# Six steps' output products of the fifth token group put off behind the last group's first layer

## The chip, the cores and the metric

The kernel runs on one core of a Trainium2 chip. The metric is device time in microseconds (us), lower is better. Three runs of the kernel before took 541.68 us in the median (541.45 to 542.41). Five engines work side by side: TensorE (PE, with its weight loads shown as PEld), VectorE (DVE), ScalarE (ACT), GpSimd (POOL), and SyncE (SP), whose queue issues the DMAs here.

## The reference

Three layers follow each other on 4 batches of 768 positions (3072 tokens of 256 values):

```python
x = attn(x, a, B, C)                                  # decay attention, chunked scan over 768 positions
h = np.maximum(np.maximum(x @ w1, x @ w2), x @ w3)    # first expert layer, 256 -> 768
x = h @ w_out                                         # 768 -> 256
h = x @ w_in                                          # second expert layer, 256 -> 2048
P = a[0] + a[1] * h + a[2] * h * h + a[3] * h * h * h
Q = 1.0 + abs(b[0]) * abs(h) + abs(b[1]) * h * h
out = (P / (Q + 1e-6)) @ w_out2                       # 2048 -> 256
```

Everything is fp32. A factor that is not exact in TensorE's fast format is split into two parts, hi and lo, and a product then takes three passes.

## The kernel before, in words

The 3072 tokens go in NG = 6 groups of T = 512 tokens (128 positions of each of the 4 batches). Each group goes through attention, the first expert layer and the second. The second is cut into 16 steps of 128 of the 2048 hidden values; step g.k below is step k of group g, both counted from 0, so the fifth group's steps are 4.0 to 4.15 and the last group's 5.0 to 5.15.

One step, written by `h_plan`, is this:

- **First layer.** Six passes of 512 columns on PE (two halves of the 256 inputs, each hi by hi, lo by hi, hi by lo; lines 856 to 858 in `mm3`) fill one PSUM bank. Called H5.4 for step 5.4.
- **Rational function.** Some 12 operations on tiles of 128x512. ACT reads the bank for `Abs` (line 1058) and a linear term (line 1056), and takes Ln and Exp (1074, 1075); POOL makes a linear term and a product (1042, 1060); DVE does the rest (1061, 1062, 1076, 1079, 1081). A second form has Square, Abs and a linear term on ACT (1065, 1066, 1069); a third, used in the last group only, copies the bank and has two products on POOL (1047 to 1053). Each works in slots A4 to A12 of SBUF; the odd steps of the last group work in slots H0 to H11, which held the first expert layer's hidden values.
- **Split.** ACT rounds the result to hi (line 1086, through the helper at line 374), POOL subtracts for lo (line 1087). Three slots each: A13 to A15 and A16 to A18.

`o_plan` then has two output products (O4.10 means both of step 4.10), three passes each, which add up over the 16 steps of a group in the two PSUM banks S2 and S3. Steps 5.6 to 5.15 use an unsplit fp32 product instead (line 1105). At the end of a group the banks are copied out and sent by DMA (lines 1123 and 1124; 1117 and 1118 for the very last step, which is done in two halves).

What sets the order: the kernel records every operation with what it reads, writes and which slot it needs, and then issues the operations engine by engine in the order of a list. That list comes from a greedy scheduler (`listed`), which reads one number per operation from a packed table, `KEYS`. Each engine runs its own list strictly in order, waiting on semaphores where an operand is not ready or a slot not free. DMAs stand in SP's list in the same way.

Of the kernel before, what the change touches and what calls it, by code (L numbers as in the profile page):

```python
# [10 lines left out]
F32 = mybir.dt.float32  # L11
F32R = mybir.dt.float32r
# [5 lines left out]
DR = bass.MemoryType.DRAM  # L18
# [6 lines left out]
T = NB * CH  # L25
# [12 lines left out]
OHALF, G0L, SPLIT = True, False, 6  # L38
# [40 lines left out]
class Plan:  # L79
# [255 lines left out]
def decay_attention_max_moe_rational_moe(  # L335
# [121 lines left out]
    def mark():  # L457
        return _Tile()
# [763 lines left out]
```

## Time and profile before

| | us |
|---|---|
| median of 3 runs | 541.68 (541.45 to 542.41) |
| the profiled execution | 541.84 |
| its span, first to last instruction | 539.70 |
| outside the span | 2.14 |
| mean granted clock of PE | 0.999 of full speed |

The profile is of one execution. Its page gives the busy time of each engine as a share of the span; views of the trace give the same in any window, the rows of one engine in order of time, and the chain of waits, followed back from the last instruction. In a row of an engine's timeline a bracket such as [0.56 <-ACT A L1058] is the time that the engine was idle before the row, and what ended it. An operation's printed duration on ACT, DVE and POOL can reach a little into the next one's, and so can a pass on PE (0.39 us printed, a start every 0.23 us).

### The profile page before, as it was taken

How to read it: one execution, taken by the hardware profiler on the slowest of the kernel's cores; microseconds unless marked ns; L12 is line 12 of the kernel's file. 1: busy time of each engine (PE TensorE's matmuls, PEld its weight loads, DVE VectorE, ACT ScalarE, POOL GpSimd, SP SyncE). 2: the span in 40 equal slices, each digit the busy share in tenths (PEclk: the TensorE clock that was granted, in tenths of full speed). 3: DMA queues.
4: the chain of work that ended last, by engine and by line, in shares of the span. 5: the costliest groups of instructions: out<-in, count | busy, mean ns of one | idle time of the engine just before them, and what ended most of it. 6: DMA issues, size and time to landing. Idle time of an engine off the chain costs nothing.

```text
span 539.7 us, 8473 instructions
## 1 busy us (share of the span) xinstructions
PE 529.9 (98%) x2866; PEld 413.9 (77%) x2866; DVE 488.5 (91%) x763; ACT 446.5 (83%) x772; POOL 435.5 (81%) x418
## 2 busy tenths in 40 slices
PE   9899999999999999999999999999999999999987
PEld 4466678888888888888888788888888888887743
DVE  6898999876987999999998999999989899789997
ACT  6998876747766998898988899989688788789994
POOL 1366557788888999998988889998878888689994
PEclk9999999999999999999999999999999999999999
DMA  6687844432624100010030100030000100001001
GB/s 217 222 294 259 242 151 158 151 112 85 239 99 149 60 20 1 0 40 1 1 117 0 40 2 1 0 125 12 1 1 1 39 2 0 2 1 39 1 0 39
DMA packets 17413, 39.46 MB, mean 73 GB/s; under 512 B 3123, under 2 KB 4443, under 8 KB 17371
## 3 DMA queue, kind: packets, MB, share of 16 engines
q1 hardware_dynamic: 17371, 38.94, 21.4%
q8 instruction: 22, 0.36, 0.3%
q14 instruction: 20, 0.16, 0.1%
HBM read 30.13 MB, written 8.80 MB: 72 GB/s over the span
## 4 chain that ended last, share of the span: by engine, by line
PE 87%; DVE 4%; DMA 3%; ACT 3%; SPq 1%; issue 1%; DVEq 0%; ACTq 0%
PE S L856 14%; PE S L858 14%; PE S L857 14%; PE G L856 7%; PE G L858 7%; PE G L857 7%; PE D L856 5%; PE D L858 5%; PE D L857 5%; PE S L1105 3%; PE Y L747 2%; DMA R<-in_w_dram 1%; PE S L699 1%; SPq L463 1%; DMA A<-in_bn_dram 1%; PE G L715 1%
## 5 line engine op out<-in xcount | busy, mean ns | idle before, releaser
L1087 POOL TENSOR_TENSOR A<-A,A 128x512 fp32r<-128x512 f32 x83 | 108.4, 1308 | 16.4 <-ACT A L374 15.8
L1060 POOL TENSOR_TENSOR A<-A,A 128x512 f32<-128x512 f32 x65 | 85.0, 1309 | 3.3
L1074 ACT ACTIVATE Y<-A,qc 128x512 f32<-128x512 f32 (+1 forms) x89 | 61.4, 690 | 11.8 <-POOL A L1060 8.2
L856 PE MATMUL S<-A,L 128*128 128x512 f32 x172 | 67.1, 390 | 0.2 <-ACT A L374 0.2
L857 PE MATMUL S<-A,L 128*128 128x512 f32 x172 | 67.1, 390 | 0.0
L1079 DVE SCALAR_TENSOR_TENSOR Y<-A,co,Y 128x512 f32<-128x512 f32 (+1 forms) x89 | 66.6, 748 | 0.4
L858 PE MATMUL S<-A,L 128*128 128x512 f32 x172 | 67.0, 389 | 0.0
L1076 DVE SCALAR_TENSOR_TENSOR A<-A,Y 128x512 f32<-128x512 f32 (+1 forms) x89 | 60.4, 679 | 7.1 <-ACT Y L1075 6.9
L428 POOL TENSOR_TENSOR C<-C,E 128x256 uint32<-128x256 uint32 x56 | 43.7, 796 | 25.0 <-DVE C L423 19.4
L1081 DVE SCALAR_TENSOR_TENSOR A<-A,Y 128x512 f32<-128x512 f32 (+1 forms) x89 | 60.6, 681 | 1.8
L374 ACT ACTIVATE A<-A 128x512 fp32r<-128x512 f32 x83 | 52.3, 630 | 10.6 <-DVE A L1081 6.7
L1042 POOL TENSOR_SCALAR A<-A,co 128x512 f32<-128x512 f32 (+1 forms) x69 | 55.6, 805 | 5.0 <-ACT A L1058 4.6
L1075 ACT ACTIVATE Y<-Y 128x512 f32<-128x512 f32 (+1 forms) x97 | 56.2, 581 | 2.1
L475 POOL TENSOR_TENSOR H<-X,H 128x512 fp32r<-128x512 f32 x30 | 40.2, 1342 | 10.4 <-ACT H L374 10.3
L856 PE MATMUL G<-xhi,w_hi 128*128 128x512 f32 x120 | 46.8, 390 | 0.0
L858 PE MATMUL G<-xhi,w_lo 128*128 128x512 f32 x120 | 46.7, 389 | 0.0
L857 PE MATMUL G<-xlo,w_hi 128*128 128x512 f32 x120 | 46.7, 389 | 0.0
L856 PEld LDWEIGHTS S<-A,L 128*128 128x128 f32 x172 | 32.3, 188 | 7.4 <-ACT A L374 0.7
L857 PEld LDWEIGHTS S<-A,L 128*128 128x128 f32 x172 | 32.3, 188 | 7.3 <-POOL A L1087 0.7
L858 PEld LDWEIGHTS S<-A,L 128*128 128x128 f32 x172 | 32.3, 188 | 6.7
L1056 ACT ACTIVATE A<-S,co 128x512 f32<-128x512 f32 x38 | 29.6, 779 | 3.7 <-POOL A L1087 2.1
L1071 POOL TENSOR_TENSOR A<-A,A 128x512 f32<-128x512 f32 x20 | 26.0, 1298 | 7.3 <-DVE A L1067 6.2
(247 smaller groups left out, 1561.4 us busy)
## 6 DMA issues: line engine op xcount, KB each, us to landing
R<-in_wo_dram SPq DMA_DIRECT2D x11, 512.0 KB
R<-in_w_dram SPq DMA_DIRECT2D x9, 512.0 KB
R<-in_win_dram SPq DMA_DIRECT2D x8, 512.0 KB
L<-in_xn_dram SPq DMA_DIRECT2D x6, 512.0 KB
out_dram<-A SPq DMA_DIRECT2D x10, 256.0 KB
xt_d<-L SPq DMA_DIRECT2D x4, 512.0 KB
L<-xt_d SPq DMA_DIRECT2D x4, 512.0 KB
y_d<-A SPq DMA_DIRECT2D x8, 256.0 KB
```

What stands on the lines that cost most here:

```text
L374: act.activation(out=o, in_=i, func=AF.Copy)
L856: pe.matmul(dst, wh, hi, start=first, stop=False, skip_group_check=skip)
L857: pe.matmul(dst, wh, lo, start=False, stop=False, skip_group_check=skip)
L858: pe.matmul(dst, wl, hi, start=False, stop=last, skip_group_check=skip)
L1042: pop(0.74, lambda: pool.tensor_scalar(out=f(t1), in0=f(v), scalar1=c(5), scalar2=c(4), op0=ALU.mult, op1=ALU.add), [v], [t1])
L1060: pop(1.26, lambda: pool.tensor_tensor(out=f(v), in0=f(t1), in1=f(v), op=ALU.mult), [t1], [v])
L1074: aop(0.6, lambda: act.activation(out=f(r), in_=f(v), func=AF.Ln, bias=qc), [v], [r])
L1075: aop(0.49, lambda: act.activation(out=f(r), in_=f(r), func=AF.Exp, scale=-1.0), [], [r])
L1076: dop(0.6, lambda: dve.scalar_tensor_tensor(out=f(v), in0=f(v), scalar=QC, in1=f(r), op0=ALU.add, op1=ALU.mult), [r], [v])
L1079: dop(0.67, lambda: dve.scalar_tensor_tensor(out=f(r), in0=f(w), scalar=c(0), in1=f(r), op0=ALU.add, op1=ALU.mult), [w], [r])
L1081: dop(0.6, lambda: dve.scalar_tensor_tensor(out=f(w), in0=f(v), scalar=2.0, in1=f(r), op0=ALU.subtract, op1=ALU.mult), [v, r], [w])
L1087: pop(1.26, lambda: pool.tensor_tensor(out=f(lo), in0=f(w), in1=f(hi).bitcast(F32), op=ALU.subtract), [w, hi], [lo])
```

## The change

A new constant DEFER = 6 names the last six steps of the fifth group, 4.10 to 4.15. Their hi and lo, once made, are each written to a DRAM tile (12 writes of 256 KB, line 1096 after the change) and read back (12 reads, line 1098) into slots of the H ring, and the output products read the copies that came back. For each step the slots A13 to A18 come free when the write has landed, not when the products are done. No instruction of PE, ACT, DVE or POOL is added or removed; SP gets 24 DMAs more. The table `KEYS` is a new one for all operations (`ZERO` goes with it, the number that is subtracted from each entry), so the whole order is written anew.

```diff
-OHALF, G0L, SPLIT = True, False, 6
+OHALF, G0L, SPLIT, DEFER = True, False, 6, 6
...
-    LOOK, KEEP, SCALE, ZERO = 0.2, 1.5, 97.0, 0.0
+    LOOK, KEEP, SCALE, ZERO = 0.2, 1.5, 97.0, 7.0
     KEYS = (
-        "XaLOv2LUnxDgeX*3j+B8I{+{NVgmUBoC0+M8UkGcT?76Dm;<r{-2<`)*94&jc?Kf{%m;P|s{lI(BF-+-xdLzn-UV+3xCOHYAPB(-=?EM"
...
+        "SOOFVg#o_=E&$;H83h0ZIRw)I5(OOvTm|?9+yoT`4hEwJC<bx{q6XLrc?a|dAPKhySPCTzSpu~QzR#@DX$2Puh6w2gUkF+W{t9pllnbH"
...
+    g_d = [dram.tile([2, 128, T], F32, name=f"g_d{k}") for k in range(DEFER)]
...
-        return hi, lo
+        if g < NG - 2 or last or k < F2 - DEFER:
+            return hi, lo
+        back = hhi_r((128, T), F32R), hlo_r((128, T), F32R)
+        d, there = g_d[k - F2 + DEFER], [mark() for _ in range(2)]
+        for i, z in enumerate((hi, lo)):
+            op("dma", 0.35, lambda i=i, z=z: nc.sync.dma_start(out=d[i], in_=z.t.bitcast(F32)), [z], [there[i]], size=262.0)
+        for i, z in enumerate(back):
+            op("dma", 0.35, lambda i=i, z=z: nc.sync.dma_start(out=z.t.bitcast(F32), in_=d[i]), [there[i]], [z],
+               when["h", (NG - 1) * F2] - 2.0 + 2 * (k - F2 + DEFER), size=262.0)
+        return back
```

Line numbers after the change are higher by 2 up to the split, and by 11 in `o_plan`.

PE around the last group's steps 5.0 to 5.4, before. The number in front is the instruction's place in PE's list. S2 and S3 are the banks of the output products, A13 to A18 hold hi and lo of the fifth group's results, K0 to K3 the last group's input to the layer, G_5562 is the bank of step 5.4:

```order
2276 L856 MATMUL S2_5027<-A13_5435,L4_2333 128x512
2277 L857 MATMUL S2_5027<-A16_5446,L4_2333 128x512
2278 L858 MATMUL S2_5027<-A13_5435,L4_2333 128x512
2279 L856 MATMUL S3_5036<-A13_5435,L4_2333 128x512
2280 L857 MATMUL S3_5036<-A16_5446,L4_2333 128x512
2281 L858 MATMUL S3_5036<-A13_5435,L4_2333 128x512
2282 L856 MATMUL S2_5027<-A14_5475,L4_2333 128x512
2283 L857 MATMUL S2_5027<-A17_5487,L4_2333 128x512
2284 L858 MATMUL S2_5027<-A14_5475,L4_2333 128x512
2285 L856 MATMUL G_5562<-K0_5375,win_hi_98 128x512
2286 L857 MATMUL G_5562<-K1_5383,win_hi_98 128x512
2287 L858 MATMUL G_5562<-K0_5375,win_lo_99 128x512
```

The products of steps 4.12 and, in part, 4.13 stand ahead of H5.4. The same engine and place after the change, where G_5573 is the bank of step 5.4, S1_5541 that of 5.3, and H1 and H6 hold what was read back for step 4.11:

```order
2267 L858 MATMUL S1_5541<-K2_5444,win_hi_104 128x512
2268 L859 MATMUL S1_5541<-K3_5470,win_hi_104 128x512
2269 L860 MATMUL S1_5541<-K2_5444,win_lo_105 128x512
2270 L858 MATMUL S2_5052<-H1_5479,L3_2270 128x512
2271 L859 MATMUL S2_5052<-H6_5502,L3_2270 128x512
2272 L860 MATMUL S2_5052<-H1_5479,L3_2270 128x512
2273 L858 MATMUL S3_5060<-H1_5479,L3_2270 128x512
2274 L859 MATMUL S3_5060<-H6_5502,L3_2270 128x512
2275 L860 MATMUL S3_5060<-H1_5479,L3_2270 128x512
2276 L858 MATMUL G_5573<-K0_5366,win_hi_104 128x512
2277 L859 MATMUL G_5573<-K1_5377,win_hi_104 128x512
2278 L860 MATMUL G_5573<-K0_5366,win_lo_105 128x512
```

H5.4 now stands behind the products of 4.11, at place 2276 in place of 2285.

ACT at the end of the fifth group, before (in the same order of names: A15 and A13 get hi of steps 4.14 and 4.15, G_5562 is the bank of step 5.4, D_5520 that of 5.3):

```order
691 L374 ACTIVATE A15_5548<-A7_5419 128x512
692 L1074 ACTIVATE Y1_5539<-H1_5546,qc_108 128x512
693 L374 ACTIVATE A13_5560<-A8_5465 128x512
694 L1056 ACTIVATE H2_5569<-D_5520,co_89 128x512
695 L1058 ACTIVATE H3_5575<-D_5520 128x512
696 L1075 ACTIVATE Y1_5539<-Y1_5539 128x512
697 L1056 ACTIVATE A7_5584<-S1_5506,co_89 128x512
698 L1058 ACTIVATE A4_5590<-G_5562 128x512
699 L1056 ACTIVATE A8_5598<-G_5562,co_89 128x512
```

Seven instructions stand between hi of 4.14 (691) and the Abs of step 5.4 (698). The same after the change, where A13 and A14 get hi of 4.14 and 4.15, G_5573 is the bank of step 5.4, D_5506 that of 5.1:

```order
686 L376 ACTIVATE A13_5551<-A7_5453 128x512
687 L1076 ACTIVATE Y0_5556<-A5_5521,qc_114 128x512
688 L1077 ACTIVATE Y0_5556<-Y0_5556 128x512
689 L376 ACTIVATE A14_5570<-A8_5476 128x512
690 L1068 ACTIVATE Y1_5580<-D_5506,co_95 128x512
691 L1060 ACTIVATE A4_5590<-G_5573 128x512
692 L1058 ACTIVATE A7_5598<-S0_5524,co_95 128x512
693 L376 ACTIVATE A15_5602<-A9_5515 128x512
694 L1058 ACTIVATE A8_5611<-G_5573,co_95 128x512
```

The Abs of step 5.4 now stands at place 691, where hi of 4.14 stood, and both hi copies stand ahead of it.

SP's list after the change, where g_d3, g_d4 and g_d5 are the DRAM tiles of steps 4.13, 4.14 and 4.15 (before, none of these rows is there):

```order
144 L1096 DMA g_d4_91<-A13_5551 128x512
145 L1098 DMA H8_5568<-g_d3_90 128x512
146 L1096 DMA g_d5_92<-A14_5570 128x512
147 L1096 DMA g_d4_91<-A16_5582 128x512
148 L1098 DMA H1_5600<-g_d4_91 128x512
149 L1096 DMA g_d5_92<-A17_5592 128x512
150 L1098 DMA H2_5619<-g_d5_92 128x512
```

The read of lo of 4.13 (145) stands behind the write of hi of 4.14 (144) in the queue.

## Rows read from the trace of the kernel before

**Rows 1.** Page, busy time, share and instructions of each engine.
```profile
PE 529.9 (98%) x2866; PEld 413.9 (77%) x2866; DVE 488.5 (91%) x763; ACT 446.5 (83%) x772; POOL 435.5 (81%) x418
```

**Rows 2.** 20-us windows: length, busy PE, PEld, DVE, ACT, POOL, clock, DMA share, GB/s.
```profile
460.00:480.00 20.00, 20.00 (x90) 16.57 (x89) 15.01 (x24) 15.30 (x26) 15.21 (x14) 1.00 0.01 2
480.00:500.00 20.00, 19.77 (x88) 15.94 (x87) 19.69 (x31) 19.59 (x36) 18.45 (x17) 1.00 0.07 26
500.00:520.00 20.00, 18.32 (x74) 13.50 (x74) 18.77 (x30) 19.06 (x33) 19.60 (x19) 1.00 0.00 1
520.00:540.00 20.00, 16.65 (x50) 7.93 (x48) 15.98 (x29) 11.53 (x24) 12.29 (x14) 0.96 0.08 26
```

**Rows 3.** The chain of waits from 483 us: start us, us, what.
```profile
483.68 0.24 PE S L858
...
483.94 0.60 ACT A L1058
...
505.17 0.69 DVE H L1061
...
513.65 0.67 DVE A L1053
...
514.37 0.50 PE G L856
...
536.73 0.42 DVE A L376
```

**Rows 4.** Timeline of PE, the last group's first layer: start us, us.
```profile
480.80 0.39 PE L858 MATMUL G<-K,win_lo 128*128 128x512 f32 x1
...
487.82 0.39 PE L856 MATMUL G<-K,win_hi 128*128 128x512 f32 x1
...
488.96 0.39 PE L858 MATMUL G<-K,win_lo 128*128 128x512 f32 x1
```

**Rows 5.** Timeline of ACT, end of the fifth group and after.
```profile
481.24 0.60 ACT L1058 ACTIVATE A<-G 128x512 f32<-128x512 f32 x1
...
482.58 0.60 ACT L1065 ACTIVATE H<-S 128x512 f32<-128x512 f32 x1
483.08 0.78 ACT L1069 ACTIVATE H<-S,co 128x512 f32<-128x512 f32 x1
...
486.13 0.64 ACT L374 ACTIVATE A<-A 128x512 fp32r<-128x512 f32 x1
...
487.34 0.63 ACT L374 ACTIVATE A<-A 128x512 fp32r<-128x512 f32 x1
...
490.20 0.60 ACT L1058 ACTIVATE A<-G 128x512 f32<-128x512 f32 x1
...
503.82 0.83 ACT L1056 ACTIVATE H<-S,co 128x512 f32<-128x512 f32 x1
```

**Rows 6.** Timeline of DVE, the first operation of step 5.9 on it.
```profile
505.17 0.69 DVE L1061 TENSOR_TENSOR H<-S,H 128x512 f32<-128x512 f32 x1 [0.83 <-ACT H L1058]
```

**Rows 7.** Timeline of POOL, waits before the last group and POOL's last operation.
```profile
470.37 2.66 POOL L1087 TENSOR_TENSOR A<-A,A 128x512 fp32r<-128x512 f32 x2 [3.26 <-ACT A L374]
...
482.01 0.77 POOL L1042 TENSOR_SCALAR A<-A,co 128x512 f32<-128x512 f32 x1 [0.52 <-ACT A L1058]
...
484.72 0.77 POOL L1042 TENSOR_SCALAR A<-A,co 128x512 f32<-128x512 f32 x1 [0.56 <-ACT A L1058]
...
532.21 0.73 POOL L1052 TENSOR_TENSOR A<-A,A 128x256 f32<-128x256 f32 x1
```

**Rows 8.** Timeline of SP's queue, a write to DRAM and the read behind it.
```profile
134.93 1.05 SPq L968 DMA_DIRECT2D y_d<-A  x2
137.59 0.32 SPq L979 DMA_DIRECT2D A<-y_d  x1
```

**Rows 9.** The chain of waits at 38 us: a 256 KB load under load.
```profile
38.58 5.43 DMA A<-in_bn_dram
```

**Rows 10.** Window of 4 us with that load, columns as in rows 2.
```profile
40.00:44.00 4.00, 3.94 (x76) 2.84 (x76) 3.25 (x8) 3.99 (x8) 1.69 (x3) 1.00 1.00 330
```

More of the change, by code (lines that the diff above doesn't have):

```diff
@@ new lines @@
+        "IxD&?g)HJN4lRf;YB3-#d@sy1a51zkpD@5LATJOxr!ILfnlk<|KQxUp{V}>SiZfI(>@f#2?l7w}4>8#|_cQ7<{xilkr8dMfh%-GlEjIx"
+        ";4mjdCNdue%<pk*hg$0rbQweYhX$%JqmkkFB)CtrHi3xBES_nA_N(s9Lr2^OmxCVL$Q3n47;0JaG_69}=mj^!x=>~uYJO~2`rUoJiNea"
+        ";m0t}T3?g#e=-Uww1#t1VAZwlWDQV4_z@(I2QhY9ZqrV9BA9195yxC?v?LJeRL>l0=XWDXAx8V?~6@(@iCWeVvEehX#{To3yV{0)>2S_"
+        "=dWF$@t6atyBxRSnh*-3)CF4h<{~!wotM;|#M7st%+MD-Wy@NfN#izz)$3fDP6Shz-~cX$>w9@(#Ka9S=SZ_zrLn4iT^r?-J$`ZV_P+y"
+        "Al%<-4o&yHW7>ug%8OPYY-<85E7^oi4P$Umk+EEoezBv+YqV{+7OQr!Ve}8FcM)Aoe}jAT@cg~-4c@(U=|@4I}`2^K@eOKI1*P9!V<O<"
@@ new lines @@
+        "jS{aCO%gd1mJ{F;A{5yZ+7(9@0vX{HITb(^FBk_Jc^9`9suh+Msudp>0~2l&;TK~RV-u7U;1t6Xt`ubz_7hwb&=#f?!xiBbUlf29aTQ<"
+        "`JrocYkQ-eb>K!B$lNk6F4i_XC0~qrb92cw?7Z}zSdKa-67a3U@85+(Uj~nS8@fxff?iuqRUmr9X_ZY+(eHmIBaUHuG*Bp)-WEKb+uNs"
+        "jUF&R=D1Q{?I<QhB~=NZcybsFOu^cwpYsvE!_8X!d>9wD6@&KsT@%Ni#gup2@eBp=`#;2pmmM;*i*k{m@JG9EY~)gdQ0ZygyO=p3dWf*"
+        "-9P>>l48$sVj9`5piqogg707$CtO#vptlI3x5RaUMz@4I|MXR3O|ZW+B@kLMap^wjmQM9V-4P_&1?C6G;U(B{#G;bvU#)0y%d%f;xXXr"
+        "#l2X4LRC40Xio-<~dtBv^#`4V>{tK#X!qCaXo`P+dB6<dqD|2A3(7{RzAT%Jw2{F)IB{x+&vjRR6xx?2tWoxPeFx2NI!-_mOytx=0eLt"
@@ new lines @@
+        "s6r1y1x71H4@S5~R74X*l|%VP&_&%v8Aj4Z#7DhJ`$>XIlSRr#6-bmvCr8akYD^eQF-z1-$V&lD|3=wKs!NGZ`%DZ_{ZMC7Yf&Uuepr5"
+        "8Xb^i6R~4lf02iYc`We9)z!;Dj#2Q)}l_5SLjv>|`ej^4Vxgs$n3?ZE(?jvL*up#Cn7bK}9<|ObXRU|ehlO&lY=Os%giYHMi_$T}(p(j"
+        "8o^(R3owI|mqaw#?{uPDkYYbv)XjVZP%aV!2Te=3qI`YeYlm@A1Z*etFsdnc_Z7%3VlEiI)jSS^<=MlLTdY%G#5A}t&+0WLW%^)Rw6S2"
+        "1)g(k?GB9x*R4^)7}mVliMbxiZc%Co<+Us4=cFa5O$Ltue<jzB2<eB{V%UHa6ijh%ibt{4wh>d^aaGW;fk6pf}<)Wi_idKQ_=efj7)J>"
+        "^N^a(l(PfP&n{5xH*tGQ#vR*^g>@nDl(lkBQ#bvPB<_*syfy=c{`yxP(4~bx;j)k0z23|AUs<<(mW_VnLyDz%RF{HPCS`A<UplCen96w"
@@ new lines @@
+        "$3Ct;$Ui|sK0=T}<3Ue9qCp@*2||%V^FdTY%R{a}mqFb^m_wdJs6^C3B}QsQ4MuQARYbBz2Sy`D)<=Fu3rB-PIYxs;wnvahb4P?mgGio"
+        "9Wk~cm*f<h6Y&ZotJvx6n(m8rP5<FHura$FLSV%KW14?Z;+&C&aQ#xTg(K??yBSqIl^F=a7fkv)M6-uH?_eoAW07BnCCqTGD2SEry`a+"
+        "jORzlB2@kQ-PkxQ9Mh)jb;I7v`N^+S?K0!qS4X-LdSr%6>y@JcOB2}}u1MNSP#Z%S-Naz@WbAWX(fBue^A$w?wj@=PgB<V{>n%S|mww@"
+        "fxn`b@-3(o8N*PEGwwIZS6wZB6-2cTmw#lTT+zt4sb&woMXGl})2h8&9cE>rdoQdr$;W0#eXX%~AbJXH5l8^G<M2IZi52T2LoYUr}gK@"
+        "KF9y&rx_&P*eR(`%f88`A&LJZBZ&wQc>Jd3{t&OQ&THZe^U)r2UV3%*iisd!%|96s#5w@%Th#AlT)QrPE%i1F;<gR99KwBq*Gi}4^yU8"
@@ new lines @@
+        "g~)Tr*2xpeV8&d?P0A0*_sI3hg~@x$sLF`SzsPXP+sGTq(#k-^dc*F;*Tp8qeZ(=x-^aSfu*ieRs>qkgP0iiMC%`So;=-H7kjE#+f5(l"
+        "+*2hW5aL6Faf6U*?*vwJIC&vuN4#>U9HOV*0jLAjIP|J16@5@}uA<ccntjLMRf5|b+vB}iRsmmG3I?L6{!OZ^3l+J0%C&@g>vdO#0I?E"
+        "EwThHUmpUj-f8q6Wk6VFD^A;+l6HO<${lg#MI)Xd||`O6Z{Y0l=$-p<v~k<anU|I4||FU(iXInDCXywPOO=gdUTY0nhTZOy{UWX_Jt!p"
+        ")D&3Cyd`*vt9NiPx*rz0cXt7Sq_wsLepnfzRU3)XhrIh|a#xSJZ&eS<hn9g3YMUNXrw`)y)&pTF&~;BGPZxQqD5Z&DR;ukkI?oGSG$5q"
+        "SoHcOwvEjHqcYjR@#=%o6cU>=h3RpP0<+EBGu2<Gt{!vpw*euu+aV1")
```

102 lines of the change are left out of this document (39 added, 63 removed).

## The prediction

> **What bounds the kernel now.** I read the page's first part first: PE is busy for 529.9 of 539.7 us, ACT, DVE and POOL for 81 to 91% [rows 1]. An average says little here, so next come the windows of 20 us where the change lies. PE is full in 460 to 480, 0.23 us short in 480 to 500, 1.68 us short in 500 to 520; in the same two windows DVE, ACT and POOL have 19.69, 19.59, 18.45 and then 18.77, 19.06, 19.60 us of 20 [rows 2]. So the bound moves from PE to the other three near 480 us. The chain of waits says the same: it lies on PE until 483.92, then on ACT and DVE until 514.32, then on PE, which after 514.37 does the last products one behind the other [rows 3]. Between 484 and 514 us what counts is therefore when the operations of the rational function get through ACT, DVE and POOL, and PE only as far as it feeds them.
>
> **What the change removes and adds.** It removes nothing. It adds 24 DMAs of 256 KB on SP's queue, and it moves instructions on all engines. In the first 480 us PE is full or nearly so and keeps its passes; the swaps there I put at 0 (bounds −0.4 and +0.4 us, about two passes, since each moves an operation past one or two others).
>
> **Term 1, PE.** Its work is the same, so it gains only what it stood still for: at most 0.23 + 1.68 = 1.91 us [rows 2]. It would earn that if the other three engines were fed earlier and could use it. H5.0 to H5.3 come three places earlier, 0.68 us, and H5.4 nine places earlier (2276 for 2285). A pass takes 0.227 us (H5.4's first and sixth stand 1.14 us apart [rows 4]), so H5.4 starts at 487.82 − 2.04 = 485.78 and ends, as before, 1.53 us later (488.96 + 0.39 − 487.82 [rows 4]): 487.31.
>
> **Term 2, ACT, on which my forecast rests.** In ACT's list the Abs of step 5.4 moves further than H5.4 does: it takes the place that hi of 4.14 had before, and that began at 486.13 [rows 5]. Its bank is not full by then. The nearest handover of this kind is H5.0, whose last pass ends at 480.80 + 0.39 = 481.19 [rows 4], and its Abs began at 481.24 [rows 5], 0.05 later. So the Abs of 5.4 can start at 487.36, not at 486.13: ACT, which runs its list in order, stands for up to 1.23 us, and 30 further instructions stand behind it up to the linear term of step 5.9. Before, the 31 instructions from hi of 4.14 on took 503.82 − 486.13 = 17.69 us [rows 5], with at most 20 − 19.59 = 0.41 us idle in that window [rows 2]. After, the 31 are the same but that two hi copies (0.64 + 0.63) went ahead and the Square and linear term of step 5.1 (0.60 + 0.78 [rows 5]) came in: +0.11. With 0.30 of the idle time gone (between none and 0.41), 487.36 + 17.69 + 0.11 − 0.30 = 504.86 us, where before it was 503.82: +1.04 (from +0.93 to +1.34).
>
> What stands behind that: DVE's first operation of step 5.9 waited 0.83 us for ACT before and began at 505.17 [rows 6], 1.35 us behind the linear term; now at 506.21. From there on the lists of ACT, DVE and POOL are nearly as before, and the chain runs through DVE to 514.32 [rows 3]. DVE's own idle time between 500 and 520 was 20 − 18.77 = 1.23 us [rows 2], of which 0.83 is this wait, so 0.40 is left to take some of it up. The end moves by +0.64 to +1.04; I take +0.7, near the lower end, because the DVE operations ahead of step 5.9 get the longer wait to catch up in.
>
> **Term 3, POOL.** It has about one operation of work behind another from 484.72 to 532.94 (532.21 + 0.73). The waits that earlier first layers can take away are 0.52 at 482.01 and 0.56 at 484.72, both for an Abs of the last group's first steps [rows 7]: −1.08 at best. The product of step 5.1 gets a new wait in their place, since 5.1's linear term on ACT now stands behind the Abs of 5.4. Net I take 0, which leaves term 2 to decide.
>
> **Term 4, the DMAs.** Issuing them is SP's work and covered. What can cost is a read that comes late for PE. The last tight one is lo of step 4.13. Its read is queued behind the write of hi of 4.14, which ACT makes behind the Abs of 5.2: H5.2's last pass (place 2263, nine after H5.0's last at 480.80) ends at 483.23, Abs and hi copy take 0.60 and 0.64 [rows 5], the write's issue about 0.5 (1.05 for two [rows 8]): 485.0. O4.13 is due on PE at 488.5 (place 2288, 34 passes behind 480.80). A write of 256 KB and the read behind it stood 2.66 us apart in the trace (134.93 to 137.59 [rows 8]): by that the copy is there at 487.7, in time, cost 0. A 256 KB load took 5.43 us on the chain [rows 9] in a stretch where the DMA engines were busy through whole windows [rows 10]: by that it is there at 490.4, and PE stands 1.9 us. I take 0, because the 12 writes and 12 reads, 6.3 MB in some 23 us, are about 270 GB/s, below the 330 of that window [rows 10], and other transfers there take a share of 0.00 to 0.07 [rows 2]; the other end stays for the range.
>
> Of this the Trainium skill says in its page DMA: Bandwidth & Descriptors, section Latency and other measured facts, that an access to HBM takes 0.2 us on average and 2 us at high load, and that this is the main part of a DMA's fixed cost. That speaks against the change, since its reads come while its own writes load the HBM. The light and the loaded row, 2.66 and 5.43 us, differ as the rule has it, though other things can make them differ too. By the light case the sum stays; by the loaded one it is the rival D below.
>
> **Sum.** 0 + 0.7 + 0 + 0 against the profiled execution's 541.84 us (span 539.70 and 2.14 outside): 542.5 us. The profiled run lies 0.16 above the median of 541.68, so against the median: 542.4 us. A difference of under 0.2% (1.08 us) can't be told from no change; faster means below 540.60, slower above 542.76.
>
> **The cases.**
>
> A, the forecast: ACT waits for H5.4, +0.4 to +1.3 us, 542.1 to 543.0, most likely 542.4. Chance 0.41, of which 0.26 lies within 0.2% and 0.15 above.
>
> B, nothing in sum, 541.2 to 542.1. The change hardly does what it says: the products of 4.11 (the second), 4.12 and on stood behind H5.0 to H5.3 before as well, so one product alone goes behind those four. The wait of ACT is then made good by the two hi copies done ahead of it and by POOL's 1.08 us. Against it: the copies are in the sum already, and ACT's 31 instructions had only 0.41 us to give. Chance 0.20, all within 0.2%.
>
> C, faster: the last group's elementwise work is fed earlier and the engines use it. POOL's two waits go, 541.68 − 1.08 = 540.6; at the far end PE's gaps all go, 541.68 − 1.91 = 539.8; about 540.2 in the middle. For it: the bound does lie with POOL, DVE and ACT from 484 us on, and POOL waited 3.26 us for a hi copy near 467 to 470 [rows 7], in the stretch that is rearranged. Against it: the Abs of 5.4 can't come before 487.31 whatever POOL does. Chance 0.18.
>
> D, slower by one late read: lo of 4.13 takes the loaded 5.43 us. PE then ends O4.13 at 488.5 + 1.9 + 6 passes (1.36) + 0.2 = 491.95. Slot H0 is free only then, and ACT's linear term of step 5.3, seventh in the list of 31, would have begun near 490.8 (487.36 and six instructions of 0.57): it waits 1.15 more. 0.7 + 1.15 = +1.85, 543.5 us against the median. It decides from the point where the read takes over 3.5 us (488.5 − 485.0), and costs ACT from about 4.3 us on. For it: the queue's write and read follow each other closely. Against it: the load is lighter than in the window of the 5.43 us. Chance 0.21.
>
> **Chances.** Faster 0.18 (C); the same 0.46 (B 0.20, A 0.26); slower 0.36 (A 0.15, D 0.21). The range of 540.4 to 543.6 us takes in A and B, the near part of C and most of D, about 8 in 10; A's own range is 542.1 to 543.0.
>
> **What the profile after would show.** Term 1: H5.4 near 485.8 us, PE without a gap before it. Term 2: a wait on ACT for PE at the Abs of step 5.4, near 487.3 us, and the linear term of step 5.9 near 504.9; if that term comes at 503.8 or before, term 2 is wrong. Term 3: POOL's waits near 482 and 485 gone or shorter, and a new one before the product of step 5.1. Term 4: reads that land within about 3 us and no gap on PE before the products of 4.13; a gap there, and an ACT wait before step 5.3 that ends with it, would be D. The forecast as a whole is wrong if the gap of 1.68 us on PE near 514 gets smaller, or if the first 480 us shift by more than 0.4 us.

## The result, and the profile after

The changed kernel took 545.06 us in the median of 4 runs (544.22 to 546.27), the kernel before 541.61 (541.45 to 542.41, 4 runs). The ratio is 1.0061, 95% interval 1.0039 to 1.0083: slower by 3.45 us. Forecast were 542.4 us and a range of 540.4 to 543.6. Twelve later runs of the same changed kernel gave 545.21 beside 541.78 before (experiment 9, ratio 1.0053, 1.0034 to 1.0073).

The profiled execution after took 544.86 us, its span is 542.8. Marks of the two traces, start times on PE in us:

| mark | before | after |
|---|---|---|
| first product of step 0.5 | 196.67 | 195.47 |
| H4.11 | 451.10 | 451.11 |
| H5.4 | 487.82 | 486.07 |
| H5.14 | 514.37 | 516.13 |
| last product | 536.06 | 539.08 |

H4.11 serves as the zero of times below ("at 46.68" is 46.68 us after H4.11 began), since the starts of two executions differ by up to some us. From step 0.5 to H4.11 the new order takes 255.63 us where the old one took 254.43 (+1.20); from H4.11 to H5.14 65.02 for 63.26 (+1.76); from H5.14 to the last product 22.95 for 21.69 (+1.26). The first 195 us were 1.20 shorter in this pair. The sum, +3.02, is what the last product is late by.

The windows of 20 us after, with the columns of [rows 2]:

```profile
460.00:480.00 20.00, 20.00 (x90) 16.56 (x89) 17.68 (x27) 15.55 (x26) 16.37 (x15) 1.00 0.37 120
480.00:500.00 20.00, 19.54 (x84) 15.26 (x83) 18.02 (x28) 18.95 (x33) 18.26 (x17) 1.00 0.63 209
500.00:520.00 20.00, 17.57 (x72) 13.75 (x71) 19.53 (x31) 19.10 (x34) 19.55 (x18) 0.94 0.04 14
520.00:543.00 23.00, 19.67 (x58) 9.84 (x56) 17.28 (x31) 12.91 (x26) 13.50 (x16) 0.98 0.07 23
```

Against [rows 2], DVE has 2.67 us more work in 460 to 480 and is 1.67 short in 480 to 500; PE is short of 0.46 and 2.43 us in the middle two windows, where it was short of 0.23 and 1.68. The DMA share of 480 to 500 went from 0.07 to 0.63. The clock is 0.94 in 500 to 520.

The chain of waits after (start us, us, what), which answers to [rows 3]:

```profile
487.37 0.24 PE G L860
487.63 0.60 ACT A L1060
488.23 0.75 ACT A L1058
489.00 0.70 DVE A L1063
...
491.65 0.75 DVE A L1064
492.44 0.50 PE G L858
...
497.52 0.24 PE S L860
...
497.79 0.02 ACT A L376
497.81 0.24 issue
498.28 1.15 ACT A L376 x2
...
505.68 0.67 ACT H L1058
...
515.42 0.67 DVE A L1055
516.13 0.50 PE D L858
...
517.57 0.43 PE D L860
...
539.75 0.42 DVE A L378
```

In [rows 3] the chain leaves PE at 483.92 and returns at 514.37. After, it leaves at 487.61, comes back to PE at 492.44 (H5.6, H5.7, and behind them the put-off products of 4.14 and the first of 4.15), and goes on to ACT only when the last pass of that product is through at 497.76. That second stay on PE is new.

The rows of PE after, with those of H5.4, of the last passes for step 4.14 (496.68) and for the first product of 4.15 (497.36), and of H5.14, and the clock behind it (start us, us, operation, idle time before it and what ended it):

```profile
486.07 0.39 PE L858 MATMUL G<-K,win_hi 128*128 128x512 f32 x1
...
496.68 0.39 PE L860 MATMUL S<-H,L 128*128 128x512 f32 x1
...
497.36 0.39 PE L860 MATMUL S<-H,L 128*128 128x512 f32 x1
...
516.13 0.50 PE L858 MATMUL D<-K,win_hi 128*128 128x512 f32 x1 [2.04 <-DVE A L1055]
...
517.17 0.41 PE L859 MATMUL D<-K,win_hi 128*128 128x512 f32 x1
517.40 0.60 PE L860 MATMUL D<-K,win_lo 128*128 128x512 f32 x1
517.80 0.63 PE L858 MATMUL S<-A,L 128*128 128x512 f32 x1
```

The wait for H5.14's bank is 2.04 us for 1.68. From 517.80 a pass starts every 0.43 us, where 0.227 is the rate of [rows 4]. The windows of 2 us there show the granted clock (the third number from the end):

```profile
516.00:518.00 2.00, 1.87 (x7) 1.55 (x8) 2.00 (x5) 1.97 (x4) 1.92 (x3) 0.85 0.00 0
518.00:520.00 2.00, 2.00 (x6) 1.52 (x6) 2.00 (x4) 1.60 (x3) 2.00 (x2) 0.50 0.00 0
520.00:522.00 2.00, 2.00 (x6) 1.10 (x5) 2.00 (x4) 1.08 (x2) 1.90 (x4) 0.79 0.00 0
```

It is 0.50 of 2.4 GHz, the lower of the two levels (1.2 GHz), some 1.3 us after the gap, and up again before 522.

ACT after, the rows that answer to [rows 5], with two that are not there, the Square of step 5.5 (497.11) and the copy of the fifth group's first output bank (497.79):

```profile
487.63 0.60 ACT L1060 ACTIVATE A<-G 128x512 f32<-128x512 f32 x1 [0.23 <-PE G L860]
...
497.11 0.60 ACT L1067 ACTIVATE H<-S 128x512 f32<-128x512 f32 x1
497.79 0.60 ACT L376 ACTIVATE A<-S 128x512 f32<-128x512 f32 x1
...
505.55 0.80 ACT L1058 ACTIVATE H<-G,co 128x512 f32<-128x512 f32 x1
```

The Abs of step 5.4 waited 0.23 us for PE; the linear term of 5.9 is 1.73 us later than in [rows 5]. DVE after, with the row of [rows 6] (506.93), and the copy of the other output bank, which waits for PE as well:

```profile
499.83 0.69 DVE L378 COPY A<-S 128x512 f32<-128x512 f32 x1 [0.56 <-PE S L860]
...
506.93 0.69 DVE L1063 TENSOR_TENSOR H<-G,H 128x512 f32<-128x512 f32 x1 [0.16 <-ACT H L1060]
```

POOL after, its waits in the stretch of [rows 7]:

```profile
469.30 1.29 POOL L1089 TENSOR_TENSOR A<-A,A 128x512 fp32r<-128x512 f32 x1 [0.81 <-ACT A L376]
472.74 1.29 POOL L1073 TENSOR_TENSOR A<-A,A 128x512 f32<-128x512 f32 x1 [2.14 <-DVE A L1069]
...
480.49 0.77 POOL L1044 TENSOR_SCALAR A<-A,co 128x512 f32<-128x512 f32 x1 [0.54 <-ACT A L1060]
...
494.33 1.30 POOL L1073 TENSOR_TENSOR H<-H,H 128x512 f32<-128x512 f32 x1 [0.90 <-ACT H L1071]
```

SP after, the write of hi of 4.14 and the read of lo of 4.13, the pair that the prediction took to be tight:

```profile
485.02 0.32 SPq L1096 DMA_DIRECT2D g_d<-A  x1
485.39 0.43 SPq L1098 DMA_DIRECT2D H<-g_d  x1
```

In 460 to 520 us no row of PE after names a DMA as what ended a wait.

### The profile page after: what moved, and what is told of

The parts are those of the page before. It is cut to its first block, busy times and chain, and to the rows that moved or that the text cites. A ratio compares the mean times of both kernels' runs of the same rounds, so it can differ in the third digit from the quotient of the medians.

```text
span 542.8 us, 8526 instructions
## 1 busy us (share of the span) xinstructions
PE 531.6 (98%) x2866; PEld 414.7 (76%) x2866; DVE 490.5 (90%) x763; ACT 445.7 (82%) x772; POOL 435.8 (80%) x418
## 4 chain that ended last, share of the span: by engine, by line
PE 72%; DVE 8%; ACT 5%; POOL 4%; issue 2%; DMA 1%; ACTq 0%; DVEq 0%; POOLq 0%
PE S L858 11%; PE S L859 11%; PE S L860 11%; PE G L858 7%; PE G L859 7%; PE G L860 7%; PE D L858 4%; PE D L860 4%; PE D L859 4%; PE S L1116 3%; POOL A L1089 1%; DVE Y L1081 1%; DVE A L1063 1%; DVE A L1064 1%; DMA R<-in_w_dram 1%
## 5 line engine op out<-in xcount | busy, mean ns | idle before, releaser
L1062 POOL TENSOR_TENSOR A<-A,A 128x512 f32<-128x512 f32 x65 | 84.4, 1301 | 3.2
L859 PE MATMUL S<-A,L 128*128 128x512 f32 x160 | 62.8, 392 | 0.0
L858 PE MATMUL S<-A,L 128*128 128x512 f32 x160 | 62.8, 392 | 0.0
L860 PE MATMUL S<-A,L 128*128 128x512 f32 x160 | 62.7, 392 | 0.0
L430 POOL TENSOR_TENSOR C<-C,E 128x256 uint32<-128x256 uint32 x56 | 45.0, 819 | 21.5 <-DVE C L425 15.8
L1044 POOL TENSOR_SCALAR A<-A,co 128x512 f32<-128x512 f32 (+1 forms) x69 | 53.7, 778 | 4.8 <-ACT A L1060 4.2
L1058 ACT ACTIVATE A<-S,co 128x512 f32<-128x512 f32 x43 | 33.5, 779 | 7.0 <-POOL A L1089 4.4
L859 PEld LDWEIGHTS S<-A,L 128*128 128x128 f32 x160 | 30.3, 190 | 6.5 <-POOL A L1089 0.2
L858 PEld LDWEIGHTS S<-A,L 128*128 128x128 f32 x160 | 30.3, 189 | 6.3
L860 PEld LDWEIGHTS S<-A,L 128*128 128x128 f32 x160 | 30.3, 190 | 6.3
L1064 DVE SCALAR_TENSOR_TENSOR A<-A,co,S 128x512 f32<-128x512 f32 x43 | 32.0, 744 | 2.7 <-ACT A L1060 1.8
```

Source lines behind the costliest of these rows:

```text
L858: pe.matmul(dst, wh, hi, start=first, stop=False, skip_group_check=skip)
L859: pe.matmul(dst, wh, lo, start=False, stop=False, skip_group_check=skip)
L860: pe.matmul(dst, wl, hi, start=False, stop=last, skip_group_check=skip)
L1044: pop(0.74, lambda: pool.tensor_scalar(out=f(t1), in0=f(v), scalar1=c(5), scalar2=c(4), op0=ALU.mult, op1=ALU.add), [v], [t1])
L1062: pop(1.26, lambda: pool.tensor_tensor(out=f(v), in0=f(t1), in1=f(v), op=ALU.mult), [t1], [v])
```

## The experiments

**How the order was edited.** In most of these kernels `KEYS` holds, for every operation, its place in its engine's list, and the scheduler may take only that one next. With the lists of the kernel before, or of the changed one, this gives the same instruction streams as those kernels.

```diff
+        turn = dict.fromkeys(wait, 0)
...
                 for j in w:
+                    if key[j] != turn[e]:
+                        continue
...
+            turn[e] += 1
             wait[e].remove(j)
```

Times of one execution are compared by stretches, since the first 195 us vary from run to run more than the effects looked for: step 0.5 began between 194.1 and 199.0 us in 20 profiled executions of all kernels.

**Which part of the order costs.** Four runs join the two orders at cuts where the same work has been done in both. 1: the old order to H4.11, then the changed one, with its DMAs. 2, and again 12: the changed order to 195 us, the old one behind it, no DMAs. 14: the changed order to H4.11, the old one behind it. In each list of before, for run 1:

```diff
 (places up to H4.11, each engine: as before)
-(places from H4.11 on: as before)
+(places from H4.11 on: as in the changed kernel, 24 DMAs)
```

> Every engine keeps the order of before up to about 451 us and has the changed order (with the 24 DMAs) from there on. Theory (the loss comes from the last 90 us): 544.5 to 545.2 us, H5.14 near 516.1 and granted clock under 1.00 between 516 and 522 us, as in the changed kernel. Rival (the loss was already laid down by the order of the first 451 us): nearer 541.7.

> The changed order up to about 195 us, the order of before from there on, no spill and no reload. In the changed kernel's trace PE stands 1.20 us ahead of before between 95 and 195 us and has lost it by 451. Theory: the lead is real and is kept where PE has no new gaps, and as the end of the kernel hangs on the whole chain, the time falls by 0.6 to 1.2 us, to 540.4 to 541.0. Rival (the elementwise engines set the end and give nothing back): 541.4 to 541.9.

> The changed order up to about 195 us and the order of before from there once more, for a narrower interval: 541.39 against 542.12 in the last comparison, ratio 0.9977 to 1.0011. Theory (the first 195 us differ from run to run by more than the two orders do): ratio within 0.998 to 1.001, 541.2 to 542.2. Rival (the changed order is better by the 1.2 us that the first two traces showed): ratio under 0.998.

> The changed order up to about 451 us and the order of before from there, no spill. Theory (the two stretches add up): 255.6 to 256.0 us from O0.5 to H4.11 as in the changed kernel, then 84.9 to 85.1 us to the last output product as in before. Rival (a late PE is made up for, or costs more, in the tail): 84.7 or less, or 85.3 or more.

| run | us (runs) | ratio to before | step 0.5 to H4.11 | H4.11 to H5.14 | to last product |
|---|---|---|---|---|---|
| before | 541.84 (profiled) | | 254.43 | 63.26 | 84.95 |
| after | 544.86 (profiled) | | 255.63 | 65.02 | 87.97 |
| 1, changed tail | 544.42 (11) | 1.0033 (1.0010 to 1.0055) | 254.44 | 65.15 | 88.07 |
| 2, changed to 195 | 541.39 (12) | 0.9994 (0.9977 to 1.0011) | 254.49 | 63.28 | 85.06 |
| 12, the same | 541.47 (12) | 0.9984 (0.9970 to 0.9999) | 254.47 | 63.26 | 84.98 |
| 14, changed to 451 | 545.90 (1) | | 255.99 | 63.78 | 85.56 |

The stretches add up like parts, but for 0.5 to 0.6 us in run 14. The tail brings about +1.8 us, and more behind H5.14. The order between 195 and 451 us brings another: over all profiled executions it is 254.33 to 254.49 us in 7 with the old order and 255.63 to 256.02 in 13 with the new (medians 254.43 and 255.81, +1.38). The changed order up to 195 us costs nothing and may gain a little (the mean of 541.39 − 542.12 and 541.47 − 541.78 is −0.5 us, and neither interval reaches far from 1); run 12 is the one version slightly ahead of both kernels.

Where the 1.38 us sits in the middle can be read from the windows, here of before and then of after:

```profile
200.00:220.00 20.00, 20.00 (x90) 16.26 (x89) 18.89 (x30) 17.64 (x31) 19.58 (x18) 1.00 0.00 1
220.00:240.00 20.00, 20.00 (x90) 16.47 (x89) 19.40 (x31) 17.48 (x31) 18.43 (x18) 1.00 0.04 13
300.00:320.00 20.00, 20.00 (x87) 15.86 (x86) 19.79 (x32) 17.69 (x32) 18.08 (x16) 1.00 0.03 11
```

```profile
200.00:220.00 20.00, 19.85 (x88) 16.02 (x87) 18.53 (x30) 17.36 (x31) 19.48 (x18) 1.00 0.00 1
220.00:240.00 20.00, 19.75 (x87) 16.05 (x86) 18.71 (x29) 17.65 (x31) 18.10 (x17) 1.00 0.04 13
300.00:320.00 20.00, 19.85 (x88) 15.97 (x87) 19.63 (x31) 17.67 (x31) 17.73 (x16) 1.00 0.00 1
```

PE is full before and not quite after. Two of the places, rows of PE after:

```profile
233.08 0.50 PE L858 MATMUL S<-A,win_hi 128*128 128x512 f32 x1 [0.25 <-DVE A L1064]
...
304.97 0.50 PE L858 MATMUL D<-xhi,w_hi 128*128 128x512 f32 x1 [0.15 <-DVE A L1064]
```

Each such wait costs more than its bracket. The pass at 233.08 starts 0.41 us later than the usual spacing of 0.227 would have it, as the printed 0.39 of the pass ahead reaches 0.16 into the wait, and the next pass (233.41) comes another 0.11 late: 0.52 us for a bracket of 0.25. Counted in this way, with all starts more than 0.03 us behind the usual spacing, PE stands 1.79 us in eleven pieces between step 0.5 and H4.11 after, and 0.58 in seven before: +1.21, against the +1.20 of this pair. Three waits make up 1.37 of the 1.79 (at 201.90, 233.08 and 304.97), and in all three PE waits for DVE to give back a bank. The other rows name no cause.

**The transfers.** 4: each write is issued twice, and each read gets a second DRAM-to-DRAM copy beside it.

```diff
+ lambda: nc.sync.dma_start(out=d2[i], in_=z.t.bitcast(F32))
...
+ lambda: nc.sync.dma_start(out=d2[2 + i], in_=d[i])
```

> The changed kernel with each of the 12 writes made twice and 12 more copies from DRAM to DRAM of 256 KB each in the same places of the queue, so 48 transfers for 24. Theory (the transfers are covered, the order costs the time): within 0.5 us of the changed kernel's 545.1. Rival (loaded transfers come late or slow the engines): 546 us or more.

553.97 us (6 runs), ratio 1.0235 (1.0209 to 1.0261): the rival of this expectation, not its theory. PE waits for reads, and the window they fall in is full:

```profile
486.26 0.49 PE L864 MATMUL S<-H,L 128*128 128x512 f32 x1 [1.42 <-DMA H<-g_d]
...
491.08 0.79 PE L865 MATMUL S<-H,L 128*128 128x512 f32 x1 [4.33 <-DMA H<-g_d]
```

```profile
480.00:500.00 20.00, 13.89 (x52) 10.35 (x50) 11.00 (x17) 11.17 (x20) 11.93 (x11) 0.83 1.01 359
```

So the profile would show a late read if there were one. The transfers of the change are covered at a share of 0.63; twice as many are not.

**The clock behind H5.14.** 3: the changed kernel, with eight passes of zeros behind H5.13, added to the output bank. 10: the same in kernel 1. 5: the kernel before with one operation of DVE in step 5.7 done twice, to make the gap before H5.14 longer. 9: the changed kernel itself once more.

```diff
+            if s == NG * F2 - 3:
+                for _ in range(8):
+                    pe.matmul(acc[0]..., zw, zw[:, None, :].to_broadcast([128, 4, CH]), start=False, stop=False, ...)
```

```diff
-        dop(0.6, lambda: dve.scalar_tensor_tensor(out=f(w), ...
+        dop(0.6, lambda: [dve.scalar_tensor_tensor(out=f(w), ...) for _ in range(2 if last and k == 7 else 1)], ...
```

> The changed kernel with 8 more passes on PE (zero times zero, added to an output bank) in the gap of 2.04 us ahead of H5.14. Theory (the clock of PE falls to 1.2 GHz after this gap, and its passes of 0.43 us cost 1.2 us): no fall of the granted clock, 543.5 to 544.0 us. Rival (PE waits for the other engines there anyway, the slow passes are covered): 545.0 within 0.4.

> The kernel before with one DVE operation (line 1081 of step 5.7) done twice, which lengthens PE's gap ahead of H5.14 from 1.68 to about 2.3 us and changes nothing else. Measured on the stretch from the start of H4.11 to the start of the last output product, 84.96 us in before and 85.06 in the run with the early order. Theory (a gap of some 2 us takes the clock down): granted clock under 1.00 behind the gap, the stretch longer by 0.6 plus 1.2 to 1.6, so 86.8 to 87.2 us. Rival (the clock fell for another reason than the gap): 0.6 us longer, 85.6, clock 1.00.

> The changed kernel itself once more, for how often the clock falls in it and for its time beside before on one chip. The mean granted clock of each run tells the fall (0.997 or less against 0.999 or 1.000): 4 of 4 runs so far, 4 of 27 of before, 7 of 11 with the changed tail alone, none of 11 with PE kept busy. Theory (falls come in a share of the runs wherever PE's gap ahead of H5.14 is some 2 us, and cost 1.6 us): falls in over half, those runs 1.2 to 2 us above the others; 544.5 to 545.5 in the median. Rival (the clock is no matter for the time): no difference between the two kinds of run.

> The order of before to about 451 us, the changed tail, and 8 passes of zeros in the gap ahead of H5.14. Theory: no fall of the clock, and of the 3.0 us that the changed tail costs 1.4 are left, so 0.8 to 2.0 us above before (ratio 1.0015 to 1.0037), and 1 us under the tail alone (544.42). Rival (the clock's passes are covered): as the tail alone, 2.3 above before.

With the zeros the clock stays up in all 11 runs of kernel 3, and H5.14 to the last product takes 21.33 us for 22.95; H5.14 itself is where it was (65.04). Kernel 9, the very same program as after, is the cleanest pair: its profiled execution has a gap of 2.06 us and no fall.

```profile
518.10 0.50 PE L858 MATMUL D<-K,win_hi 128*128 128x512 f32 x1 [2.06 <-DVE A L1055]
```

```profile
518.00:520.00 2.00, 1.90 (x8) 1.60 (x9) 2.00 (x5) 1.97 (x4) 1.92 (x3) 1.00 0.00 0
520.00:522.00 2.00, 2.00 (x8) 1.32 (x8) 2.00 (x4) 1.60 (x4) 2.00 (x2) 1.00 0.00 0
```

H5.14 at 65.01, the last product at 86.34 instead of 87.97: a fall costs 1.63 us. The other traces bear this out. Of the 12 with the changed tail and no zeros, the clock falls behind H5.14 in six (after, 1, 7, 13, 17, 18) and stays up in six (4, 6, 8, 9, 11, 15). From H5.14 to the last product the first six take 22.91 to 22.95 us and the others 21.32 to 21.37, with gaps of 2.02 to 2.07 us in both. By the mean granted clock of a run it fell in 7 of those 12 runs of kernel 9 (median 545.48, the other five 544.53) and in all 4 of the first comparison; in runs of the kernel before in 4 of 27 and 4 of 29. In kernel 1 it fell in 7 of 11 runs, and in kernel 10, with the zeros, still in 2 of 12. The mean does not say where it fell: the trace of run 14 has a fall at 27.86 us and that of run 4 one at 487.72, so these counts can take in falls elsewhere. Kernel 5 says that the gap's length alone does not decide: 2.37 us, and the clock at 1.00 (H4.11 to the last product 85.44 us, near the rival's 85.6). The run medians do not show the gain that the zeros should bring: kernel 3 took 544.61 (11 runs, ratio 1.0050, 1.0033 to 1.0067), kernel 10 543.48 (12 runs, 1.0031, 1.0009 to 1.0052), neither apart from its twin. The price of a fall, some 1.6 us, is known from traces, not from medians.

**What sets H5.14.** My reason was the place of step 5.4's Abs in ACT's list, so 8 puts it behind the two operations that followed:

```diff
-ACT: Abs 5.4 / linear 5.2 / hi 5.0
+ACT: linear 5.2 / hi 5.0 / Abs 5.4
```

> The changed kernel with one move on ACT: the Abs of step 5.4 stands behind the linear term of 5.2 and hi of 5.0, right ahead of 5.4's own linear term, so ACT no longer stands for H5.4. My prediction's step 2 (the place of this Abs costs about 1 us): H5.14 comes 0.8 to 1.2 us earlier than 65.02 us after H4.11. Rival (the trace after shows only 0.23 us of waiting ahead of it, since ACT came there late): at most 0.25 us earlier.

H5.14 at 65.39, no gain (last product 86.76, 543.92 us). The linear term of 5.2 could not use the place, since its slot was still being read by POOL:

```profile
488.47 0.78 ACT L1062 ACTIVATE A<-S,co 128x512 f32<-128x512 f32 x1 [0.79 <-POOL A L1093]
```

H4.15 is 1.65 us later than before (25.45 for 23.80), so 6 puts it two products earlier, 7 four, and 11 moves the rest of step 4.15 along with it.

```diff
-PE: O4.9 (both) / H4.15
+PE: H4.15 / O4.9 (both)
```

> The changed kernel with one move on PE: H4.15 stands ahead of the two products of step 4.9 and not behind them, 1.36 us earlier. Theory (the elementwise engines lose their 1.7 us between 474 and 484 us because the first layer of 4.15 comes late): ACT's waits there shrink, H5.14 comes 0.4 to 1.2 us earlier after H4.11 than the 65.02 us of the changed kernel, and if the gap falls under 2 us the clock stays up and 1.3 more are won. Rival (my prediction's step: ACT waits for H5.4, which doesn't move): H5.14 stays at 65.0 us after H4.11.

> The same with H4.15 also ahead of the last two products of the first expert layer, 2.72 us earlier. Theory: as before or up to 0.4 us better, unless those products, now later by 1.36 us, hold up H5.0. Rival: 65.0 us.

> The changed kernel with the products of 4.9 and H4.15 ahead of the last two products of the first expert layer on PE (H4.15 1.36 us earlier, and the slot of hi of 4.13 free 1.36 us earlier as well), and on ACT and DVE the work of 4.15 ahead of the copy of that layer's output. Theory (ACT's waits between 474 and 484 us cost the 1.7 us, all that stands behind them is ACT's full list): ACT's lag behind before at the linear term of 5.0 falls from 1.47 to about 0.6, and H5.14 comes 64.2 to 64.6 us after H4.11 in place of 65.02. Rival (the lag comes back through POOL or DVE): 64.9 or more.

H5.14 at 65.49, 65.58 and 65.64 (545.63, 547.46, 543.42 us): each a little worse. Then less work: 13 leaves out the Exp of steps 5.0 to 5.2 on ACT, 15 adds the move of 8, 16 leaves the same out of the kernel before; 17 leaves out POOL's product of step 5.2, 18 adds the move of 8.

```diff
-        aop(0.49, lambda: act.activation(out=f(r), in_=f(r), func=AF.Exp, scale=-1.0), [], [r])
+        aop(0.49, lambda: None if last and k < 3 else act.activation(...), [], [r])
```

> The changed kernel without the Exp (line 1077) of steps 5.0, 5.1 and 5.2, three ACT instructions that take some 0.5 us each; their results are not those of the reference. Theory (from 484 us on the changed kernel's end hangs on ACT's full list): H5.14 comes 1.0 to 1.5 us earlier, 63.5 to 64.0 us after H4.11. Rival (POOL or DVE set the pace there, ACT only shows full): at most 0.5 earlier, 64.5 or more.

> The changed kernel with the Abs of step 5.4 behind the linear term of 5.2 and hi of 5.0 on ACT (as e8) and without the Exp of steps 5.0, 5.1 and 5.2 (as e13; results not the reference's). Theory (two walls of one height, ACT's list and the Abs that stands for H5.4): H5.14 comes 0.5 to 1.2 us earlier than in e13, 63.9 to 64.6 us after H4.11. Rival (another wall: POOL, or the products of 4.14 and 4.15 on PE that ACT's Square of 5.5 and copy of the output wait for): 64.8 or more.

> The kernel before without the Exp of steps 5.0, 5.1 and 5.2 (results not the reference's). In its trace the chain runs through ACT and DVE from 484 us on. Theory (before hangs on ACT there, without a second wall at the same height): H5.14 comes 0.6 to 1.5 us earlier than 63.26 us after H4.11. Rival (a second wall there as well, DVE's or POOL's list): at most 0.4 earlier.

> The changed kernel without POOL's product (line 1062) of step 5.2, 1.3 us just ahead of lo of 4.14 (results not the reference's). Theory (two walls: the Abs that stands for H5.4 remains): the linear term of 5.2 still begins near 488.1, H5.14 comes at most 0.4 us earlier than 65.02 us after H4.11. Rival (POOL alone sets the pace, the place of the Abs is no matter): 0.7 to 1.3 earlier, 63.7 to 64.3.

> The same with the Abs of step 5.4 behind the linear term of 5.2 and hi of 5.0, as in e8 (results not the reference's). Theory (both walls gone): the linear term of 5.2 begins near 487.4, 0.8 us earlier, and H5.14 comes 0.5 to 1.0 us earlier than in the changed kernel, 64.0 to 64.5. Rival (the end does not hang on this linear term): 64.8 or more.

H5.14 at 65.08, 65.43, 63.25, 65.13 and 64.98. In 18 the linear term of 5.2 does begin 0.86 us earlier, and the end does not move. Taken alone or in these pairs, neither less work on ACT or POOL, nor the place of the Abs or of H4.15, makes the end come earlier. With the Abs later, the wait moves to PE: the gap before H5.6 is 0.55 us in 8 and 0.62 in 18, for 0.25 after.

What all these runs share came out of laying their marks side by side. E is the end of PE's last pass for the first product of step 4.15, which closes the fifth group's first output bank; C is the start of ACT's copy of that bank; all from H4.11:

| run | E | C | H5.14 | H5.14 − C |
|---|---|---|---|---|
| before | 40.96 | 43.95 | 63.26 | 19.31 |
| after | 46.64 | 46.68 | 65.02 | 18.34 |
| 8, Abs later | 47.01 | 47.05 | 65.39 | 18.35 |
| 11, step 4.15 earlier | 47.26 | 47.29 | 65.64 | 18.34 |
| 13, less ACT | 46.69 | 46.73 | 65.08 | 18.35 |
| 18, less POOL, Abs later | 46.60 | 46.64 | 64.98 | 18.34 |
| 4, DMAs doubled | 56.84 | 56.87 | 75.22 | 18.35 |

In all 14 executions with the changed tail the copy begins 0.03 to 0.04 us after E, and H5.14 18.34 to 18.35 us after the copy, even where late reads move E by 10.2 us (run 4). With the old tail the copy begins 2.99 us after E and waits for ACT alone. So H5.14 moves with E: the copy moves by +2.73 us, the list behind it is 0.97 shorter, together +1.76. The chain of after shows the same step (497.52, 497.79, 498.28). That the first output bank is closed late is the change itself: three products of 4.14 and 4.15 now follow H5.5 to H5.7 on PE, and H5.6 first waits for a bank that the rational function of 5.4 has to free.

The copy is not the only operation that waits for these products. Just ahead of it in ACT's list stands the Square of step 5.5. It writes slot H1, in which the read-back hi of 4.14 lay, and in all 14 executions it begins 0.04 us after the end of PE's last pass for 4.14 (497.11; the pass of 496.68 ends at 497.07). Where ACT has less to do, in run 13, the wait shows in the row:

```profile
496.67 0.60 ACT L1067 ACTIVATE H<-S 128x512 f32<-128x512 f32 x1 [0.50 <-PE S L860]
```

DVE's copy of the other bank waits as well, for the second product of 4.15: 0.54 to 0.59 us in 13 executions, 3.01 in run 4. From that copy to H5.14 the rows of DVE after name one wait only, of 0.16 us for ACT (506.93). PE's products for 4.14 and 4.15 thus reach H5.14 by two ways, one through ACT and one through DVE, and the first is the longer one by only some 0.16 us.

How much these waits cost can be estimated. After, ACT came to the Square only some 0.2 us early: it starts 0.87 us behind the operation ahead, and the same pair of starts is 0.66 apart at 493.45. The copy starts 0.68 us behind the Square, where 0.47 is usual (490.13). Together that is 0.4 us of the +1.76. ACT was late before it came to them: the Abs of 5.4 starts 1.50 us later than the hi copy that had its place (487.63 for 486.13).

Not tried: these three products ahead of H5.5, or the copy later in ACT's list. By the two ways above, the second should gain little more than 0.16 us, as DVE's way stays. The link between E and H5.14 is seen in 14 executions, its removal in none, so how much of the +1.76 would go with it stays open.

## Why the prediction was wrong

- **"In the first 480 us PE ... keeps its passes" (0, at most ±0.4): failed.** The new order costs +1.38 us between 195 and 451 us, in short waits of PE; in the trace after, three of them, for DVE to free a bank, make up 1.37 us, and no run shows why DVE came late there. I took PE full in the windows as a sign that it would stay so; it was full by a margin of nothing, and the list of every engine was new.
- **Term 1: right.** H5.4 at 486.07 for 485.78, no gap before it. PE earned nothing from it, as assumed.
- **Term 2: the sign and the start right, the sum behind it short.** The Abs of 5.4 began at 487.63 for the 487.36 predicted, as soon as H5.4 was through, though ACT stood only 0.23 us for it and not up to 1.23, as it came there later itself. The 31 instructions from there on took 17.92 us, where the sum had 17.50, so the linear term of 5.9 was at 505.55 for the 504.86 predicted. The missing 0.42 is about what the Square of 5.5 and the copy of the output bank waited for the put-off products: I followed ACT's list from the Abs on without asking when each operation's operands and slots would be ready on PE. None of it was made good on DVE: its wait went from 0.83 to 0.16 us and H5.14 moved by +1.76, where I had given it +0.7. That the Abs began near its forecast does not show that its place cost the time; 8 and 18, which moved it, gained nothing.
- **Term 3: nearly right.** The wait near 485 is gone, that near 482 is still there (0.54 at 480.49), and the new one before the product of 5.1 came (0.90 at 494.33). Run 17 says that POOL did not decide.
- **Term 4: right.** The read of lo of 4.13 was issued at 485.39, for the 485.0 predicted, and cost nothing. The rule of the Trainium skill quoted there (DMA: Bandwidth & Descriptors, Latency and other measured facts: 0.2 us to HBM on average, 2 us at high load) would have spoken for rival D. At the share of 0.63 the trace shows no wait that it would explain; at 1.01, in run 4, reads came up to 4.33 us late, which no run splits into latency and queueing.
- **No term for the clock: missing.** A fall costs 1.63 us and by the mean clock came in 11 of 16 runs after, about 1.1 us in the mean, where the kernel before had it in 8 of 56. I read the 1.68 us gap as idle time and nothing else. The 0.96 in 520 to 540 of [rows 2] was no sign of it: the clock is 1.00 from 520 to 536 and falls at 538.59, after PE's last pass (start 536.32).

The account, from traces: +1.38 (195 to 451 us), +1.39 (H4.11 to the last product with the clock up, 86.34 − 84.95), +1.1 less 0.2 for the falls of before (8 of 56), −0.5 from the first 195 us: about +3.2, measured +3.45. The first 195 us are its loosest term, so that the sum comes this near is partly luck. The prediction's signs of failure (the gap near 514 us, a shift of the first 480) named the right places; the first was given as one that would get smaller, and it grew.

## What to carry to other kernels

When work of one engine is put off, look up every operation of the other engines that consumes its last result or needs a slot that it still reads, here a copy out of an accumulating bank on ACT, another on DVE and a Square that needs slot H1: on an engine that runs its list in order, each holds up everything behind it. Where PE is full with no slack, do not put a wholly new order at zero: price a few short waits. And price a gap on PE with the clock behind it, not only its own length.

## What the runs showed of the hardware

- The same program, with the same gap of 2.04 and 2.06 us, had the clock at 0.50 behind it in one execution and at 1.00 in another; in 12 traces with gaps of 2.02 to 2.07 us it fell in six, and with 2.37 us (run 5) it stayed up. What decides is open. The Trainium skill's page TensorE: Matmul & The Clock Gate, Part 1, has the clock follow how busy PE has been recently; the runs agree in that zeros in the gap mostly keep it up (21 of 23 runs), and do not tell the two executions apart.
- A pass behind a short wait is itself long: 0.50 us printed and 0.33 to 0.34 to the next start, where 0.39 and 0.227 are usual. A wait costs about 0.27 us more than its bracket: 0.1 for this pass, and 0.16 by which the printed duration of the pass ahead reaches into the wait (0.52 for 0.25 at 233.08).
- 24 transfers of 256 KB in some 23 us stay hidden at a DMA share of 0.63 (209 GB/s); with the extra copies, 1.01 (359 GB/s) made PE wait 1.42 and 4.33 us.
- The start of step 0.5 moved by up to 4.9 us between executions, for kernels of both orders (194.1 to 199.0), while the 254 to 256 us from there to H4.11 repeat within 0.2 us in the old order and 0.4 in the new.
